# Late pieces of a filter's forward transform in three fp16 products, and a new order at the end of a prologue

## The chip, the cores and the metric

One Trainium2 chip, of which the program uses one core. The metric is the device time of one execution in microseconds (us), as the median of several runs.

## The reference

Two independent computations on 2048 x 448 inputs, whose results stand side by side. A is attention with 16 query heads of 28 columns and one head of keys and values. B is a filter: a real 2D FFT over rows and columns, a product with complex weights, and the inverse FFT.

```python
q = (x @ wq).reshape(B, S, 16, 28).transpose(0, 2, 1, 3)
k, v = x @ wk, x @ wv
p = softmax(einsum("bhqd,bkd->bhqk", q, k) * 28 ** -0.5)
a = einsum("bhqk,bkd->bhqd", p, v).transpose(0, 2, 1, 3).reshape(B, S, 448) @ wo
b = irfft2(rfft2(x) * (w_r + 1j * w_i), s=(S, D))
return concatenate([a, b], axis=-1)
```

## The kernel before

**Prologue** (lines 230 to 720). The projections of A, and the first part of the filter for pieces 0 to 4. Its tasks are given to a planner (`Plan`, line 45) that puts each engine's tasks in an order by their costs and due times; PE's tasks keep the order in which they are written. At its end PE does, in written order, the features of piece 4 (`fa_task(4, 0)`), a small product for the largest bound (`tops`), transposes of half of the values (`first_values`), the products of piece 3 (`fm_task(3)`), and `last_values` (line 628): a register load of `bits` on every engine, the second features unit of piece 4, and the other transposes. Behind it stands a branch on that register (line 646), whose body isn't run with these inputs.

**Main loop** (from line 1280). 256 steps: 16 groups (4 chunks of 512 queries by 4 groups of 4 heads) by 16 blocks of 128 keys. `scores` does half a step, eight fp16 matmuls into two PSUM banks (line 1258) and one exp of 128 x 1024 on ACT (line 1261); `values` does one step, four fp32 matmuls (line 1277; the profile counts an fp32 matmul as two). Three pairs of banks serve the scores, so PE can be up to three score groups ahead of ACT, and up to nine exps may lie ahead of the values. Banks 6 and 7 take the values of one group in turn; the other one of the two is free for other products, the fillers. At a group's end DVE evicts its bank (`group_out`, line 1148).

**Fillers.** What else PE has to do stands in four queues (`work`): late pieces of the filter ("l"), the filter's last part ("z"), output products of A ("w", "more"). `filler` and `fill` put one into the loop when its share is owed. DVE's own work is put in order by a clock that the kernel keeps while it is being written (`after`, `vector`): an event is written out when that clock reaches it. All this is settled before the program runs. On the chip each engine works its list in order and waits for what it needs.

**Late pieces.** The forward transform is cut into 8 pieces of 256 columns (two of them units p = 0, 1). Pieces 5 to 7 are done in the main loop, and the second half of piece 4. For each piece DVE folds its input (`late_fold`, three parts), PE does two features units (`late_features`, 16 fp32 matmuls of 32 x 113 at line 173), DVE copies each out of PSUM (line 1013), PE does two points units (`late_points`, 8 fp32 matmuls of 32 x 226 at line 1026), DVE copies them to `bs` (line 1035), and SP stores them to DRAM (line 196). The inputs of piece 7 are loaded when piece 6 has left their place. When piece 7 is stored, `spectrum` begins the rest of the filter: transform, weights and inverse on DVE, then the z products on PE.

**Round trips.** A largest value over all partitions is found by a store of 128 columns to DRAM and a load of all of them to every partition (`bounce`, line 909: `md`, `mw`). Before the change there are two, one for scales of values and output weights (`largest`), one for the filter's spectrum.

**Queues.** SP issues the loads of inputs, the query copies (`qd`, `qa`), the stores of `bs` and the round trips, in order; POOL issues bulk loads (`wo`, filter weights `w`, `X`) and each group's sums (`sd`, `rs`, `rd`, `R`), also in order. An issue whose source or place isn't ready holds up all that stand behind it.

Of the kernel before, what the change touches and what calls it, by code (L numbers as in the profile page):

```python
# [23 lines left out]
S, D, H = 2048, 448, 16  # L24
# [20 lines left out]
class Plan:  # L45
# [56 lines left out]
def kernel(ctx: ExitStack, tc: tile.TileContext, t: dict):  # L102
# [29 lines left out]
    def spin(*dims):  # L132
        return view(bank[next(turn) % 6], *dims)

    L = 4
# [2 lines left out]
    late["w", 4] = spare[0][1][:, 1416:1928]  # L138
    for q in range(5, 8):
        (one, two), o = spare[q > 5], 452 * (q > 5)  # L140
        late["x", q], late["f", q] = one[:, :1024], one[:, 1024:]
        late["w", q], late["a", q] = two[:, o:o + 512], two[:, o + 512:o + 1416]
    for (n, q), x in late.items():
        dims = {"x": dict(k=4, n=256), "f": dict(k=4, j=4, h=2, m=32), "w": dict(h=2, j=4, m=64), "a": dict(j=2, e=2, n=226)}[n]
        late[n, q] = x.rearrange(f"p ({' '.join(dims)}) -> p {' '.join(dims)}", **dims)
    xb, ff = {}, {}
    f1 = [None]

# [15 lines left out]

    at1 = {}

    def features(pa, f, p):
        for e in range(2):
            for k in range(2):
                for h in range(2):  # L170
                    for r in range(2):
                        r0 = 64 * h + 32 * r
                        mm(pa[r0:r0 + 32, e, 113 * k:113 * k + 113], f[:113, 2 * r + k, 2 * p + e, h], cs1[:113, 2 * r + k],  # L173
                           start=True, stop=True)
# [23 lines left out]

    def late_load(q, names):
        for n in names:  # L200
            nc.sync.dma_start(late[n, q], t["xb"][q] if n == "x" else t["fz"][:, q - L])

    qa, qd = {}, {}

# [27 lines left out]
    with tc.tile_pool(name="f1", bufs=2) as f1[0], tc.tile_pool(name="w1", bufs=1) as w1, ExitStack() as ctx1:  # L232
# [232 lines left out]
            xb_load(q)  # L465

        def late_start():
            late_load(5, "xw")
            late_load(6, "xw")
# [149 lines left out]
        def tops():  # L619
            pb = small["t"] = spin(128)  # L620
            mm(pb[0:1], cmax, cons["ident"], start=True, stop=True)
        bt_ = small_bank(0.2, tops, 0.15, lambda: nc.vector.tensor_reduce(bits, small["t"][0:1], axis=AX.X, op=ALU.max),
                         cm, ident_)
        tv = add(PE, 0.6, first_values, users[-6], ident_, *krow_, *fetched["v"][:7])
        users.append(None)
        fm_task(3)

        def last_values():
            small["rv"] = nc.values_load(bits.bitcast(I32)[0:1, 0:1])
# [105 lines left out]
    def after(when, dur, f, *a):  # L735
        heapq.heappush(events, (when, next(serial), dur, f, a))
# [169 lines left out]
        V.tensor_reduce(m[:, 1:2], peaks[:, 8:16], axis=AX.X, op=ALU.max)  # L906
        bounce(m, fix_peak)

    def bounce(m, then):
        d = dp.tile([128, 2], F32, name="md", bufs=2)  # L910
        nc.sync.dma_start(d, m[:, :2])
        w = ap.tile([128, 128, 2], F32, name="mw", bufs=1)
        nc.sync.dma_start(w, d.rearrange("(o a) b -> o a b", o=1).to_broadcast([128, 128, 2]))

        def go():
            V.tensor_reduce(m[:, :2], w.rearrange("p a b -> p b a"), axis=AX.X, op=ALU.max)
            V.tensor_scalar(m[:, :2], m[:, :2], 1e-30, None, op0=ALU.max)
            then(m)
        after(clk["dve"] + 14.0, 1.0, go)

    def fix_peak(m):
        V.reciprocal(m[:, 2:4], m[:, :2])
# [70 lines left out]
    last_kind = ["w"]  # L993
    done = [0.0]

    def late_fold(q, part=0):
        fold_part(late["x", q][:113], late["f", q][:113], part)
        if part < 2:
            after(clk["dve"], (1.22, 1.4)[part], late_fold, q, part + 1)
        else:  # L1000
            if q == 6:
                late_load(7, "x")
            work["l"].extend([late_features(q, 0), late_features(q, 1)])

    def late_features(q, p):
        def go(b):
            features(view(bank[b], 2, 226), late["f", q], p)
            after(clk["pe"] + LAG, 0.6, out, b)
            if q < 7 and p:
                after(clk["pe"] + (1.8 if q == 5 else 5.0), 1.22, late_fold, q + 1)  # L1010

        def out(b):
            V.tensor_copy(late["a", q][:, p], view(bank[b], 2, 226))
            free[b] = clk["dve"] + 0.1
            after(clk["dve"] + 0.2, 0.0, work["l"].appendleft, late_points(q, p))
        return 0.86, go

    bsl = {}

    def late_points(q, p):  # L1020
        def go(b):
            pb = view(bank[b], 2, 226)
            for h in range(2):
                for e in range(2):
                    for m in (0, 32):
                        mm(pb[64 * e + m:64 * e + m + 32, h], late["w", q][:, h, 2 * p + e, m:m + 32], late["a", q][:, p, e],  # L1026
                           start=True, stop=True)
            after(clk["pe"] + LAG, 0.6, out, b)
            if q == 6 and p:
                late_load(7, "w")  # L1030

        def out(b):
            if p == 0:
                bsl[q] = fp.tile([128, 2, 2, 2, 113], F32, name="bs")
            V.tensor_copy(bsl[q][:, :, :, p], view(bank[b], 2, 2, 113))  # L1035
# [7 lines left out]
        return 0.76, go  # L1043

    def spectrum():
        t0 = clk["dve"] + 3.0
# [334 lines left out]
def _constants():  # L1381
    f = np.float32
    c = {}
    c["krow"] = np.ones((8, S))
    c["krow"][:4], c["krow"][4:] = -ROW, UP
    sel = np.zeros((128, 2, 128))
    blk = np.zeros((128, 128))
    for i in range(4):
        for d in range(DH):
            sel[32 * (d // 4 % 4) + DH + d % 4, d // 16, 32 * i + d] = 1.0  # L1390
        blk[32 * i:32 * i + DH, 32 * i + DH:32 * i + 32] = 0.25 / ROW
    c["mask"] = (np.arange(128) % 32 < DH).astype(f)[:, None]
# [30 lines left out]
    c["fw"], c["fz"] = fw[:, :16], fz.reshape(128, 4, 2, 4, 64)  # L1423
    c["fi"] = np.stack([rot(2 * np.pi * (np.outer(kp, n1) / 64 + n2 * kp[:, None] / S)) for n2 in range(32)], 1)
    c = {k: np.ascontiguousarray(v.astype(f)) for k, v in c.items()}
    for k, scale in (("fi", 64.0), ("cs3", 32.0 * D)):
        x = c[k] * f(scale)
        h = x.astype(np.float16)
        c[k] = np.ascontiguousarray(np.stack([h, (x - h.astype(f)).astype(np.float16)], 2))
    return c  # L1430


# [65 lines left out]
```

## Time and profile before

| | |
|---|---|
| median of 3 runs | 579.47 us (578.97 to 580.06) |
| the profiled execution | 579.57 us, span 577.8 |
| first scores of the main loop | 61.87 us |
| last output products begin | 564.3 us |
| granted TensorE clock | 1.0 |

Times within the profile count from the span's start. "PE" rows are matmuls, "PEld" their weight loads; a row of the timeline merges instructions of one kind that follow each other, gives start and length (the last one's tail included, so the next row's start says when PE went on), and in brackets what ended an idle time. In a group's row the two numbers behind the bar are the busy time and the mean of one in ns.

### The profile page before, as it was taken

The page shows a single profiled execution, that of the slowest core. Times are in us where ns is not written, and L with a number is a line of the kernel's source. Part 1 is how long each engine was busy: PE and PEld are TensorE (multiplying, and loading weights), DVE is VectorE, ACT ScalarE, POOL GpSimd, SP SyncE. Part 2 cuts the span into 40 slices and gives each one's busy share as a digit, 9 for nine tenths or more (in the row PEclk, how much of TensorE's full clock was granted, in tenths as well). Part 3 has the DMA queues.
Part 4 walks back from the last instruction along what each step waited for, and adds up shares of the span by engine and source line. Part 5 has one row for each costly group of instructions (what it writes and reads, how often), then busy time and mean ns, then how long its engine had stood idle before and what let it go on. Part 6 is the DMA issues. An engine that isn't in the chain of part 4 may idle for free.

```text
span 577.8 us, 20635 instructions
## 1 busy us (share of the span) xinstructions
PE 571.3 (99%) x8941; PEld 300.6 (52%) x8941; DVE 390.5 (68%) x747; ACT 513.3 (89%) x580; POOL 110.5 (19%) x199
## 2 busy tenths in 40 slices
PE   9999999999999999999999999999999999999997
PEld 7877454545554444444444444445455555555554
DVE  5996727955421999998998887854366743366544
ACT  4744899999999999999999999998999887899982
POOL 1023311212103012121201311123202321011110
PEclk9999999999999999999999999999999999999999
DMA  8864682625417102243301120457224341212111
GB/s 290 295 205 140 175 247 73 191 81 146 161 37 218 58 18 66 75 123 98 91 34 57 41 60 31 155 208 230 78 88 128 109 130 70 89 58 73 41 55 65
DMA packets 38502, 66.27 MB, mean 115 GB/s; under 512 B 7013, under 2 KB 28653, under 8 KB 38401
## 3 DMA queue, kind: packets, MB, share of 16 engines
q1 hardware_dynamic: 29576, 38.95, 21.1%
q0 software_dynamic: 8688, 25.76, 14.2%
q8 instruction: 70, 1.15, 0.8%
q14 instruction: 24, 0.19, 0.1%
q10 hardware_dynamic: 144, 0.23, 0.1%
HBM read 44.22 MB, written 19.97 MB: 111 GB/s over the span
## 4 chain that ended last, share of the span: by engine, by line
PE 72%; issue 7%; DVE 5%; DMA 3%; POOL 2%; ACT 0%; POOLq 0%; DVEq 0%; ACTq 0%
PE banks L1258 31%; PE banks L1277 30%; PE banks L1196 6%; PE banks L1094 2%; PE banks L1120 2%; DMA rd<-rs 1%; DMA wf<-w 1%; DVE X L817 1%; DVE X L818 1%; PE banks L1026 1%; POOL R L1164 1%; DVE X L859 1%; PE banks L173 0%; ACT yb L1208 0%; DVE w L852 0%
## 5 line engine op out<-in xcount | busy, mean ns | idle before, releaser
L1261 ACT ACTIVATE p<-banks 128x1024 f32<-128x1024 f32 x512 | 477.2, 1094 | 23.7 <-PE banks L1258 22.3
L1258 PE MATMUL banks<-qa,ka 128*32 128x512 f16 x4096 | 276.4, 379 | 0.4 <-PEq L646 0.4
L1277 PE MATMUL banks<-p,vs 128*32 128x512 f32 x2048 | 268.6, 592 | 0.0
L1258 PEld LDWEIGHTS <-ka 128*32 128x32 f16 x4096 | 129.5, 96 | 167.1 <-issue 119.1
L1277 PEld LDWEIGHTS banks<-p,vs 128*32 128x32 f32 x2048 | 69.9, 110 | 43.5 <-issue 1.7
L1156 POOL DMA_DIRECT2D sd<-qraw x15 | 10.1, 671 | 165.4 <-DVE qraw L1151 165.4
L1196 PE MATMUL banks<-woh,o 128*32 128x448 f16 x464 | 39.6, 353 | 0.1
L1164 POOL DMA_DIRECT2D R<-rd x60 | 30.8, 521 | 38.3 <-DMA rd<-rs 38.1
L1196 PEld LDWEIGHTS <-o 128*32 128x32 f16 x720 | 22.6, 97 | 27.4 <-issue 20.2
L859 DVE SCALAR_TENSOR_TENSOR X<-w,X 128x226 f32<-128x226 f32 (+2 forms) x72 | 34.1, 474 | 2.4
L1151 DVE TENSOR_SCALAR qraw<-banks,scales 128x512 f32<-128x512 f32 x15 | 11.3, 750 | 31.5 <-PE banks L1277 31.4
L1201 DVE TENSOR_SCALAR ya<-banks,scales 128x448 f32<-128x448 f32 x12 | 8.2, 683 | 27.5 <-PE banks L1196 27.5
L1127 DVE TENSOR_SCALAR w<-banks,scales 128x256 f32<-128x256 f32 x16 | 7.7, 484 | 27.3 <-PE banks L1120 27.3
L1162 POOL DMA_DIRECT2D rd<-rs x15 | 8.2, 549 | 90.1 <-DVE rs L1161 81.6
L1196 PE MATMUL banks<-wol,o 128*32 128x448 f16 x256 | 24.4, 352 | 0.0
L340 PE MATMUL banks<-xh,wqh 128*128 128x512 f32 x64 | 23.6, 399 | 0.0
L340 PE MATMUL banks<-xh,wql 128*128 128x512 f32 x64 | 23.0, 390 | 0.0
L344 ACT ACTIVATE qraw<-banks 128x512 f32<-128x512 f32 x16 | 9.3, 595 | 15.0 <-PE banks L340 15.0
L817 DVE TENSOR_TENSOR X<-X 128x904 f32<-128x904 f32 (+2 forms) x10 | 9.1, 906 | 16.1 <-DMA X<-t 16.1
L852 DVE SCALAR_TENSOR_TENSOR w<-X 128x113 f32<-128x113 f32 (+2 forms) x56 | 17.8, 356 | 0.1
L1035 DVE COPY bs<-banks 128x452 f32<-128x452 f32 x8 | 5.0, 619 | 18.6 <-PE banks L1026 18.5
L340 PE MATMUL banks<-xl,wqh 128*128 128x512 f32 x48 | 17.3, 390 | 0.0
(157 smaller groups left out, 553.1 us busy)
## 6 DMA issues: line engine op xcount, KB each, us to landing
qa<-qd SPq DMA_DIRECT2D x62, 128.0 KB
ob<-yo SPq DMA_DIRECT2D x16, 256.0 KB
t<-bs SPq DMA_DIRECT2D x16, 226.0 KB
w<-w POOLq DMA_DIRECT2D x8, 452.0 KB, 4.7
X<-t POOLq DMA_DIRECT2D x8, 452.0 KB, 7.1
wf<-w POOLq DMA_DIRECT2D x8, 452.0 KB, 4.0
x<-t POOLq DMA_DIRECT2D x8, 452.0 KB, 4.4
R<-rd POOLq DMA_DIRECT2D x60, 56.0 KB, 2.1
```

The lines of the kernel that those rows point to most:

```text
L340: mm(pq[c, g], w[:, j, gs], x[:, j], start=(j == 0 and n == 0), stop=(j == 3 and n == 1))
L817: todo(226 * n, lambda: TT(both(a), both(a), both(b), op=ALU.add), at)
L852: STT(out, y, sy, x, op0=ALU.mult, op1=ALU.add if c > 0 else ALU.subtract)
L859: todo(226 * n, lambda d=d, q=q: STT(both(d), t[0].rearrange("p r n f -> p r (n f)"), q, both(a), op0=ALU.mult, op1=ALU.add))
L1094: mm(pz[r, j], fb["c2", q % 2][:, x, e, j, r], fb["fi", q % 2][:, j, f], start=(n == 0), stop=(n == 2))
L1120: mm(py[m:m + 32, k].rearrange("p (j n) -> p j n", j=4), cs3[:w, kind, f, m:m + 32], fb["z", q % 2, e][:w, x, :, 64 * r:64 * r + 64], star ...
L1151: V.tensor_scalar(o, bank[b], scale_v, None, op0=ALU.mult)
L1164: nc.gpsimd.dma_start(R[32 * i:32 * i + DH], rd[i:i + 1].to_broadcast([DH, CW]))
L1196: mm(p[r:r + 32], x[c][:, g, s][:, r:r + 32], w[:, m], start=(g == 0 and n == 0), stop=(g == NG - 1 and n == 2))
L1258: mm(bank[b + h][r], ka[:, k:k + 32], qa[c, g][:, 2 * p + h], start=True, stop=True)
L1261: nc.scalar.activation(pt[i], banks[:, b:b + 2], AF.Exp, scale=SCALE / UP / UP)
L1277: mm(bank[b][32 * i:32 * i + 32], vs[:, kc], pt[2 * st + i // 2][:, i % 2], start=(kc == 0), stop=(kc == 15))
```

## The change

Pieces 5 to 7 get the fp16 form that the filter's last part has: a number x is the sum of a high part in fp16 and a low part, x less the high one, in fp16, and a product of two such numbers is three fp16 products (high by high, high by low, low by high), which are summed in PSUM.

- Constants `cs16` and `fz16` come in both parts from DRAM, scaled by 1024. The folded input is scaled by 4096 over the piece's largest input and split by DVE (`late_split`, two instructions). The features are split as they leave PSUM (two instructions in place of one copy), and the points are scaled back as they leave it.
- The largest inputs of pieces 5 to 7 are found early (`late_top`: three reduces on DVE and a third round trip, of three columns).
- Piece 7's input and weights get places of their own and are loaded at the start of the main loop, as is `cs16`.
- A features unit is 48 fp16 matmuls, a points unit 24. Points that are ready go ahead of other late work in order of coming (`late_ready`). The costs that the kernel's clock knows are changed with them, and the filter weights' largest values are asked for earlier (`weight_top` at 14 in place of 24).
- At the prologue's end `fm_task(3)` stands ahead of `first_values`, and the first half of piece 4's last features unit ahead of the register load.

```diff
+        if q < 7:
+            late["x", q], late["W", q] = one[:, :1024], two[:, o:o + 512]
+        late["f", q], late["A", q] = one[:, 1024:], two[:, o + 512:o + 1416]
+    late["C", 0] = spare[1][1][:, :452]
...
+        fm_task(3)
         tv = add(PE, 0.6, first_values, users[-6], ident_, *krow_, *fetched["v"][:7])
         users.append(None)
-        fm_task(3)
 
         def last_values():
+            pas[4, 1] = spin(2, 226)
+            features(pas[4, 1], ff[4], 1, (0,))
             small["rv"] = nc.values_load(bits.bitcast(I32)[0:1, 0:1])
-            pas[4, 1] = spin(2, 226)
-            features(pas[4, 1], ff[4], 1)
+            features(pas[4, 1], ff[4], 1, (1,))
             turn_values(range(8, 16))
...
+    def late_top(qs):
+        m = ap.tile([128, 8], F32, name="mt", bufs=1)
+        V.memset(m, 0.0)
+        for n, q in enumerate(qs):
+            V.tensor_reduce(m[:113, n:n + 1], late["x", q][:113], axis=AX.XY, op=ALU.max, apply_absolute_value=True)
...
+        bounce(m, fix, 3)
...
+    def late_split(q, n):
+        f, x, scale = late["f", q][:113], late["F", q][:113], tops[q][:113, 0:1]
+        if n == 0:
+            V.tensor_scalar(x[:, 0], f, scale, None, op0=ALU.mult)
+            after(clk["dve"], 1.25, late_split, q, 1)
+        else:
+            STT(x[:, 1], f, scale, x[:, 0], op0=ALU.mult, op1=ALU.subtract)
             work["l"].extend([late_features(q, 0), late_features(q, 1)])
+    THREE = (0, 0), (0, 1), (1, 0)
...
-            features(view(bank[b], 2, 226), late["f", q], p)
-            after(clk["pe"] + LAG, 0.6, out, b)
+                    for n, (x, y) in enumerate(THREE):
+                        for h in range(2):
+                            for r in range(2):
+                                r0 = 64 * h + 32 * r
+                                mm(pa[r0:r0 + 32, e, 113 * k:113 * k + 113], f[:113, x, 2 * r + k, 2 * p + e, h],
+                                   c[:113, 2 * r + k, y], start=(n == 0), stop=(n == 2))
...
-    after(24.0, 0.0, weight_top, 0)
+    after(14.0, 0.0, weight_top, 0)
-    after(3.0, 1.22, late_fold, 5)
-    total = 12 * 2.09 + 32 * 0.67 + 6 * 0.86 + 8 * 0.76
+    late_load(0, "C")
...
+    after(6.0, 3.4, late_top, (5, 6, 7))
+    after(6.1, 1.22, late_fold, 5)
+    total = 12 * 2.09 + 32 * 0.67 + 6 * (0.64 + 0.58) + 2 * 0.76
```

How the change moves instructions, as the two programs are written. Line numbers of the changed kernel are its own (line 173 becomes 183, 1258 becomes 1323, and so on).

PE at the end of the prologue, from the small product for the bound to the branch, before (`spol,f` are features of piece 4, `a,fw` the products of piece 3, `ident,kf` the transposes):

```order
L621 MATMUL banks<-ident,cmax 1x128
L606 MATMUL banks<-ident,kf 128x32 x8
L183 MATMUL banks<-a,fw 64x226 x8
L629 TENSOR_LOAD bits
L173 MATMUL banks<-spol,f 32x113 x16
L606 MATMUL banks<-ident,kf 128x32 x8
L646 COMPARE_AND_BRANCH
```

and of the change:

```order
L632 MATMUL banks<-ident,cmax 1x128
L193 MATMUL banks<-a,fw 64x226 x8
L617 MATMUL banks<-ident,kf 128x32 x8
L183 MATMUL banks<-spol,f 32x113 x8
L642 TENSOR_LOAD bits
L183 MATMUL banks<-spol,f 32x113 x8
L617 MATMUL banks<-ident,kf 128x32 x8
L658 COMPARE_AND_BRANCH
```

The products of piece 3 and the transposes have changed places, and eight of the features' matmuls stand ahead of the register load.

SP at the start of the main loop, behind the copies of the keys, before (`qd` and `qa` are the queries of the next group, `md` and `mw` the round trip, `t` the stores of piece 4):

```order
L215 DMA qd<-qh 128x512
L215 DMA qd<-ql 128x512
L218 DMA qa_79<-qd 32x4x512 x4
L911 DMA md<-m 128x2
L913 DMA mw<-md 128x256
L196 DMA t_83<-bs 256x1x226 x2
```

and of the change:

```order
L212 DMA spol<-cs 128x904
L212 DMA x_976<-xb 128x1024
L212 DMA W_978<-fz 128x1024
L226 DMA qd<-qh 128x512
L226 DMA qd<-ql 128x512
L229 DMA qa_79<-qd 32x4x512 x4
L923 DMA md_1092<-mt 128x3
L925 DMA mw<-md_1092 128x384
L923 DMA md_1158<-m 128x2
L925 DMA mw<-md_1158 128x128x2
L206 DMA t_83<-bs 256x1x226 x2
```

Three loads (the constants, piece 7's input and its weights) stand ahead of the queries, and the round trip of the largest inputs ahead of the one that was there.

DVE around the eviction of group 0's bank (`qraw<-banks`), before (`wo` are output weights, `qt`, `qh`, `ql` the next queries, `spol<-banks` the copy of a features unit):

```order
L768 TENSOR_SCALAR woh<-wo,scales 128x448
L770 SCALAR_TENSOR_TENSOR wol<-wo,scales,woh 128x448
L893 TENSOR_REDUCE peaks<-w 128x1
L1151 TENSOR_SCALAR qraw<-banks,scales 128x512
L207 TENSOR_SCALAR qt<-qraw,mask,cvec 128x512
L208 CAST qh<-qt 128x512
L209 TENSOR_TENSOR ql<-qt,qh 128x512
L768 TENSOR_SCALAR woh<-wo,scales 128x448
L770 SCALAR_TENSOR_TENSOR wol<-wo,scales,woh 128x448
L1013 COPY spol<-banks 128x452
```

and of the change (the first row is the low part of piece 5; the small instructions behind the second round trip stand right ahead of it):

```order
L1044 SCALAR_TENSOR_TENSOR spoh<-spoh,t_1357 113x1024
L780 TENSOR_SCALAR woh<-wo,scales 128x448
L782 SCALAR_TENSOR_TENSOR wol<-wo,scales,woh 128x448
L218 TENSOR_SCALAR qt<-qraw,mask,cvec 128x512
L219 CAST qh<-qt 128x512
L220 TENSOR_TENSOR ql<-qt,qh 128x512
L1216 TENSOR_SCALAR qraw<-banks,scales 128x512
L780 TENSOR_SCALAR woh<-wo,scales 128x448
L782 SCALAR_TENSOR_TENSOR wol<-wo,scales,woh 128x448
L905 TENSOR_REDUCE peaks<-w 128x1
L1067 TENSOR_SCALAR spol<-banks 128x452
L1068 SCALAR_TENSOR_TENSOR spol<-banks,spol 128x452
```

The eviction now stands behind the low part of piece 5 and behind the next queries, which followed it.

On PE the features units of pieces 5 to 7 stood after steps 7 and 17, 22 and 33, 37 and 50, and now stand after 18 and 19, 28 and 34, 39 and 50; their points after 11 and 19, 26 and 33, 41 and 53, and now after 20 and 22, 33 and 36, 41 and 51. The points of piece 4 stay after 0 and 4. From step 83 on (now 84) the output and z products follow in almost the same order as before.

More of the change, by code (lines that the diff above doesn't have):

```diff
@@ L140, with shaped @@
         (one, two), o = spare[q > 5], 452 * (q > 5)
[L141 to L144, printed above, removed]
+        if q < 7:
+            late["x", q], late["W", q] = one[:, :1024], two[:, o:o + 512]
+        late["f", q], late["A", q] = one[:, 1024:], two[:, o + 512:o + 1416]
+    late["C", 0] = spare[1][1][:, :452]
+    def shaped(n, q, x):
+        dims = {"x": dict(k=4, n=256), "f": dict(k=4, j=4, h=2, m=32), "w": dict(h=2, j=4, m=64), "a": dict(j=2, e=2, n=226),
+                "F": dict(x=2, k=4, j=4, h=2, m=32), "W": dict(h=2, x=2, j=4, m=64), "A": dict(j=2, x=2, e=2, n=226),
+                "C": dict(k=4, x=2, n=113)}[n]
+        if n == "x" and q > L:
+            shaped("F", q, x)
+        x = x.bitcast(F16) if n in "FWAC" else x
         late[n, q] = x.rearrange(f"p ({' '.join(dims)}) -> p {' '.join(dims)}", **dims)
+    for (n, q), x in list(late.items()):
+        shaped(n, q, x)
     xb, ff = {}, {}
@@ L165, with features @@
     at1 = {}
-    def features(pa, f, p):
-        for e in range(2):
+    def features(pa, f, p, es=(0, 1)):
+        for e in es:
             for k in range(2):
@@ L200, in late_load @@
         for n in names:
-            nc.sync.dma_start(late[n, q], t["xb"][q] if n == "x" else t["fz"][:, q - L])
+            src = t["xb"][q] if n == "x" else t["fz16"][:, q - L - 1] if n == "W" else t["fz" if n == "w" else "cs16"]
+            nc.sync.dma_start(late[n, q], src)
     qa, qd = {}, {}
@@ L994, with fix @@
     done = [0.0]
+    tops = {}
+    def late_top(qs):
[3 more added lines that the diff above has]
+            V.tensor_reduce(m[:113, n:n + 1], late["x", q][:113], axis=AX.XY, op=ALU.max, apply_absolute_value=True)
+        def fix(m):
+            for n, q in enumerate(qs):
+                tops[q] = ap.tile([128, 2], F32, name=f"t{q}", bufs=1)
+                V.tensor_scalar(tops[q][:, 1:2], m[:, n:n + 1], 1.0 / ROW, None, op0=ALU.mult)
+                V.reciprocal(m[:, 4:5], m[:, n:n + 1])
+                V.tensor_scalar(tops[q][:, 0:1], m[:, 4:5], 4096.0, None, op0=ALU.mult)
+                if q in folded:
+                    after(clk["dve"], 0.75, late_split, q, 0)
+        bounce(m, fix, 3)
+    folded = set()
     def late_fold(q, part=0):
@@ L1000, in late_fold @@
         else:
-            if q == 6:
-                late_load(7, "x")
+            folded.add(q)
+            if q in tops:
+                after(clk["dve"], 0.75, late_split, q, 0)
+    def late_split(q, n):
[5 more added lines that the diff above has]
+            STT(x[:, 1], f, scale, x[:, 0], op0=ALU.mult, op1=ALU.subtract)
@@ L1003, in late_fold @@
             work["l"].extend([late_features(q, 0), late_features(q, 1)])
+    THREE = (0, 0), (0, 1), (1, 0)
     def late_features(q, p):
         def go(b):
-            features(view(bank[b], 2, 226), late["f", q], p)
-            after(clk["pe"] + LAG, 0.6, out, b)
+            pa, f, c = view(bank[b], 2, 226), late["F", q], late["C", 0]
+            for e in range(2):
+                for k in range(2):
+                    for n, (x, y) in enumerate(THREE):
[4 more added lines that the diff above has]
+                                   c[:113, 2 * r + k, y], start=(n == 0), stop=(n == 2))
+            after(clk["pe"] + LAG, 1.3, out, b)
@@ L1009, in go @@
             if q < 7 and p:
-                after(clk["pe"] + (1.8 if q == 5 else 5.0), 1.22, late_fold, q + 1)
+                after(clk["pe"] + 1.8, 1.22, late_fold, q + 1)
         def out(b):
-            V.tensor_copy(late["a", q][:, p], view(bank[b], 2, 226))
+            a, pa = late["A", q][:, p], view(bank[b], 2, 226)
+            k = 2.0 ** -17
+            V.tensor_scalar(a[:, 0], pa, k, None, op0=ALU.mult)
+            STT(a[:, 1], pa, k, a[:, 0], op0=ALU.mult, op1=ALU.subtract)
             free[b] = clk["dve"] + 0.1
-            after(clk["dve"] + 0.2, 0.0, work["l"].appendleft, late_points(q, p))
@@ L1016, in late_features, with late_ready @@
-        return 0.86, go
-    bsl = {}
+            after(clk["dve"] + 0.2, 0.0, late_ready, q, p)
+        return 0.64, go
+    def late_ready(q, p):
+        work["l"].insert(len(points), late_points(q, p))
+        points.append((q, p))
+    bsl, points = {}, []
     def late_points(q, p):
         def go(b):
+            if q > L:
+                points.remove((q, p))
             pb = view(bank[b], 2, 226)
             for h in range(2):
[L1024 to L1027, printed above, removed]
+                for n, (x, y) in enumerate(THREE if q > L else ((0, 0),)):
+                    for e in range(2):
+                        for m in (0, 32):
+                            w, a = ((late["W", q][:, h, x], late["A", q][:, p, y]) if q > L else
+                                    (late["w", q][:, h], late["a", q][:, p]))
+                            mm(pb[64 * e + m:64 * e + m + 32, h], w[:, 2 * p + e, m:m + 32], a[:, e],
+                               start=(n == 0), stop=(n == 2 or q == L))
@@ L1034, in out @@
                 bsl[q] = fp.tile([128, 2, 2, 2, 113], F32, name="bs")
-            V.tensor_copy(bsl[q][:, :, :, p], view(bank[b], 2, 2, 113))
+            y, pb = bsl[q][:, :, :, p], view(bank[b], 2, 2, 113)
+            if q > L:
+                V.tensor_scalar(y, pb, tops[q][:, 1:2], None, op0=ALU.mult)
+            else:
+                V.tensor_copy(y, pb)
             free[b] = clk["dve"] + 0.1
@@ L1042, in out @@
                     after(clk["dve"] + 0.1, 0.0, spectrum)
-        return 0.76, go
+        return 0.58 if q > L else 0.76, go
     def spectrum():
```

32 lines of the change are left out of this document (17 added, 15 removed).

## The prediction

> **What bounds the kernel now.** I read the page's table of engines, then the windows by stage, then ACT's waits in each stage, then PE's timeline.
>
> ```profile
> PE 571.3 (99%) x8941; PEld 300.6 (52%) x8941; DVE 390.5 (68%) x747; ACT 513.3 (89%) x580; POOL 110.5 (19%) x199
> ```
>
> PE is never out of work by this count, and ACT's exps fill most of the span too. A busy PE may still stand and wait inside a group, so the next view cuts the main loop where its character changes. Columns: window, its length, then busy time and instructions of PE, PEld, DVE, ACT, POOL.
>
> ```profile
> 61.87:168.90 107.03, 107.00 (x1656) 54.07 (x1657) 64.09 (x107) 103.12 (x112) 20.60 (x38) 1.00 0.48 140
> 168.90:223.07 54.17, 54.06 (x724) 22.65 (x720) 37.26 (x62) 54.17 (x60) 12.55 (x23) 1.00 0.33 98
> 223.07:390.60 167.53, 167.53 (x2428) 77.52 (x2421) 143.04 (x312) 166.45 (x182) 30.88 (x55) 1.00 0.28 87
> 390.60:562.40 171.80, 171.80 (x3344) 92.19 (x3340) 91.47 (x155) 153.45 (x162) 31.59 (x54) 1.00 0.29 96
> ```
>
> The late pieces stand in the first stage. There ACT lacks little, in the second and third next to nothing, and only the last is plainly PE's. ACT's waits in the first and in the last stage:
>
> ```profile
> ACT p L1261 <- PE banks L1258: 4.1, 10, 1.3
> ACT p L1261 <- PE banks L1258: 18.1, 38, 1.9
> ```
>
> So whatever the change does to the late pieces can bring at most 4.1 us in their own stage. Next PE's timeline, rows from several windows:
>
> ```profile
> 77.45 0.96 PE L173 MATMUL banks<-spol,spoh 113*32 113x113 f32 x32
> 78.23 1.48 PE L1258 MATMUL banks<-qa,ka 128*32 128x512 f16 x24
> ...
> 85.12 0.95 PE L1026 MATMUL banks<-spol 128*32 128x226 f32 x16
> 85.88 1.48 PE L1258 MATMUL banks<-qa,ka 128*32 128x512 f16 x24
> ...
> 88.47 1.04 PE L1277 MATMUL banks<-p,vs 128*32 128x512 f32 x8
> ...
> 90.19 1.04 PE L1277 MATMUL banks<-p,vs 128*32 128x512 f32 x8
> ...
> 94.49 1.14 PE L1258 MATMUL banks<-qa,ka 128*32 128x512 f16 x16
> 95.44 1.04 PE L1277 MATMUL banks<-p,vs 128*32 128x512 f32 x8
> ...
> 184.96 1.04 PE L1277 MATMUL banks<-p,vs 128*32 128x512 f32 x8
> ...
> 186.79 1.04 PE L1277 MATMUL banks<-p,vs 128*32 128x512 f32 x8
> ...
> 402.97 0.86 PE L1094 MATMUL banks<-fi,c 128*32 128x128 f16 x48
> 403.64 1.05 PE L1258 MATMUL banks<-qa,ka 128*32 128x512 f16 x16
> ...
> 422.63 0.84 PE L1120 MATMUL banks<-z,cs 113*32 113x256 f16 x24
> 423.29 1.05 PE L1258 MATMUL banks<-qa,ka 128*32 128x512 f16 x16
> ```
>
> From start to start: a step without other work takes PE 1.72 us (88.47 to 90.19), and 1.83 where PE waits for exps to free banks (184.96 to 186.79). So ACT's pace is 1.83 a step and PE gains 0.11 in each step that has nothing else. A features unit costs 0.78 (77.45 to 78.23), a points unit 0.76. After the one at 85.12 PE waits again first at 94.49, five steps on (that score pair takes 0.95 and not 0.86): the lead that PE can have is some 5 x 0.11 = 0.6 us deep. A unit that is longer than the lead makes ACT wait for the rest; a step in which the lead is full makes PE wait. PE's groups follow one another without gaps, so the loop's time is **PE's work plus PE's waits**, and the sum goes by that.
>
> **The change, part by part.** All against the profiled run, 579.57 us (span 577.8), which is 0.1 above the median of 579.47.
>
> *Products.* A features unit goes from 16 fp32 matmuls of 113 columns to 48 fp16 ones. The nearest row is the unit at 402.97: 48 fp16 matmuls of 128 columns in 0.67 us, so 113/128 of it, 0.60 (between 0.59 and 0.67). A points unit goes from 8 of 226 to 24 in fp16; 24 of 256 take 0.66 (422.63 to 423.29), so 0.58. Pieces 5 to 7 have six of each: 6 x 0.18 + 6 x 0.18 = **-2.2 us**. The two points units of piece 4 stay fp32.
>
> *A wait that goes.* The first product of piece 7:
>
> ```profile
> 136.51 1.22 PE L173 MATMUL banks<-spol,spoh 113*32 113x113 f32 x29
> ...
> 137.65 1.47 PE L1258 MATMUL banks<-qa,ka 128*32 128x512 f16 x23
> ```
>
> 1.14 and not 0.78: it waited for the fold on DVE. **-0.3**; whether a new wait takes its place is below.
>
> *PE's waits for exps.* No late product now stands between steps 4 and 18. The lead is full by step 9, and nine steps wait 0.11 each: +0.9. In steps 18 to 53 about -0.1. Behind the last late product the order has 109 score and 51 value groups issued where it had 110 and 53; scores less twice the values are 7 where they were 4, so 1.5 value groups more (1.3 us) fill steps in which PE waited: -1.1. In the six rounds of 16 steps between 84 and 179 the third and fourth group of output products stand two steps apart where they stood three, so one more step per round waits: 6 x 0.11 = +0.65. Together **+0.4**.
>
> *End of the prologue.*
>
> ```profile
> 57.88 0.65 PE L606 MATMUL banks<-ident,kf 32*128 32x32 f32 x8
> 58.46 0.99 PE L183 MATMUL banks<-a,fw 64*64 64x226 f32 x16
> ...
> 59.87 0.98 PE L173 MATMUL banks<-spol,f 113*32 113x113 f32 x32 [0.41 <-issue]
> ...
> 61.87 1.21 PE L1258 MATMUL banks<-qa,ka 128*32 128x512 f16 x16 [0.40 <-PEq L646]
> ```
> ```profile
> L629 POOLq TENSOR_LOAD <-bits x1: 482/482/482, 58.1 to 58.1; - x1
> ...
> L629 PEldq TENSOR_LOAD <-bits x1: 1332/1332/1332, 58.5 to 58.5; - x1
> ```
>
> The register load takes POOL 0.48 and PE 1.33, to 59.8: 0.38 behind the end of the products ahead of it (58.46 + 0.99). It seems to wait until PE is empty, so half of the features put ahead of it delays it by as much (0.39). Fewer instructions are then left to issue before the branch (8 matmuls, about -0.2), and the store products can start as soon as the small product ahead ends, since the four waits of the transposes now pass beside them (about -0.2). **0**, between -0.4 (the load doesn't wait, the 0.41 gap is covered) and +0.3 (only the delay is real).
>
> *DVE, SP and POOL.* Rows for the new DVE work, and for the round trip through DRAM that spreads a largest value:
>
> ```profile
> L1080 DVE TENSOR_SCALAR c<-x,scales 128x904 f16<-128x904 f32 x8 | 5.5, 690 | 9.5 <-PE banks L1094 9.5
> L1081 DVE SCALAR_TENSOR_TENSOR c<-x,scales,c 128x904 f16<-128x904 f32 x8 | 9.3, 1159 | 0.7
> L893 DVE TENSOR_REDUCE peaks<-w 128x1 f32<-128x904 f32 x8 | 8.7, 1087 | 0.0
> L893 DVE TENSOR_REDUCE peaks<-X 128x1 f32<-128x1808 f32 x2 | 4.0, 2002 | 0.0
> L1013 DVE COPY spol<-banks 128x452 f32<-128x452 f32 x6 | 3.7, 624 | 8.5 <-PE banks L173 8.5
> ...
> 74.03 0.34 SPq L911 DMA_DIRECT2D md<-m  x1
> 85.74 0.34 SPq L913 DMA_DIRECT2D mw<-md  x1
> 89.05 0.44 DVE L916 TENSOR_REDUCE m<-mw 128x2 f32<-128x256 f32 x1 [2.23 <-DMA mw<-md]
> 72.43 1.59 POOL L802 DMA_DIRECT2D X<-t  x3
> 99.87 0.54 POOL L765 DMA_DIRECT2D wo<-wo  x1
> wo<-wo POOLq DMA_DIRECT2D x2, 224.0 KB, 4.7
> ```
>
> By size: three reduces 3 x 1.23, three splits 3 x (0.78 + 1.31), six second evictions 6 x 0.62, some 12 small ones of 0.17: 16 us more on DVE, which has 64.1 of the first stage's 107.0 busy. It fits; the question is when. The order has two tight places.
>
> First, step 18. The first features unit needs bank 7, which group 0's eviction frees. On DVE that now stands behind both round trips: 2.0 (some eleven small ones), 1.3 (low part), 1.1 (a weight split), 1.7 (the next queries) and 0.75 for itself, 6.8 in all. PE arrives at about 97.3 (step 16's scores at 94.49, less some 0.8 that ACT no longer waits in group 0, plus two steps), so the second trip must end by **90.5**. In before the only one took from 74.03 to 89.05, since its store landed 11.7 us later, with the bulk that POOL issues around 72.4. Now the first store goes at about 75.5, behind the loads of piece 7. The bulk goes later too, at 76 to 80, since it waits for DVE's reduces that now follow piece 7's. So the first store should land ahead of it, and the second trip end at 88 to 90. I take 0; the other end is a rival.
>
> Second, step 28, the first product of piece 6. From the end of the product of step 19 PE has 19 score and 9 value groups and two points units ahead of it: 19 x 0.43 + 9 x 0.86 + 1.2 = 17.1 us. DVE has to evict (0.25 + 1.25), then the 21 instructions up to piece 6's low part: 2 x 2.0 for X, 2 x 1.09, 2.1 for the split, and 16 of 0.25 to 0.69 for folds, copies and weights, some 16.4, or 1.2 less where they overlap. That is 16.7 to 17.9. It may also wait for the third weight load, issued at 99.87 and 4.7 us on its way. So 0 to 2; I take **+0.4**, near the lower end, since a wait there is over before the next group's queries. Piece 7's product at step 39 comes out level.
>
> The transforms on DVE and the z products behind them hang on loads at 176 to 187 behind POOL's sums of group 2; those don't move. Cost 0.
>
> Sum: -2.2 - 0.3 + 0.4 + 0 + 0.4 = -1.7: **577.9 us**.
>
> **Rivals.**
>
> *The late inputs eat the gain.* Both tight places at their middle, 1.5 us of PE standing still: 577.9 - 0.4 + 1.5 = 579.0. For it: piece 7 waited for its fold in before, and DVE now has 80 of 107 us there. Against: the new order already puts the units of pieces 5 and 6 some steps later.
>
> *Slower: the second round trip is late.* SP issues the four transfers in order, so the second trip starts only behind the first one's landing. If the first store lands with the end of POOL's bulk, as the one of 74.03 did, that is some 12 us from 76, 88; the first load comes 3.3 later (85.74 to 89.05), and the second trip, two landings of about 2 us on, at 94 to 96: 3.5 to 5.5 past the 90.5 from which it decides. Every us past it is a us that PE stands at step 18, since the unit itself uses up the lead. 577.9 + 3.5 to 5.5 = 581.4 to 583.4. Against: the bulk has moved behind the store. The Trainium skill, page "DMA: Bandwidth & Descriptors", section "Queues, rings and completion order", has the engines take turns between queues packet by packet, by which 1 KB wouldn't wait out another queue's loads; 11.7 us here speaks against leaning on it.
>
> *Slower: small matmuls have a floor.* If each fp16 matmul took a slot of its own of 25 ns, features would take 48 x 0.025 = 1.2 and points 0.6: 6 x 0.42 - 6 x 0.16 = +1.6 in place of -2.2, 581.7. The row at 402.97 has 48 of them in 0.67, 14 ns each, over four column groups, which speaks against it at 128 columns; 113 is near. The Trainium skill has this floor ("TensorE: Matmul & The Clock Gate", section "Wait — 56ns, not 53.3ns?"), for matmuls one after the other in one array.
>
> **How the numbers follow.** Forecast 0.58 (576.9 to 578.3, by the prologue's bounds and stalls of 0 to 0.8), late inputs 0.28 (578.3 to 580.4), late round trip 0.10, floor 0.04. About 0.2%, 1.16 us, is what a measurement of this kernel tells from no change. Faster by more: the forecast and little else, 0.59. Within: 0.28. Slower, over 580.6: the last two, 0.13. The range leaves out the slower mechanisms and little below: 576.9 to 580.4.
>
> **What would show it.** Right: features units of 0.60 and points of 0.58 between scores; ACT's wait in the first stage down from 4.1 to about 1.5; steps 9 to 18 at 1.83. The prologue: first scores at 61.6 to 62.1. Wrong: a features unit of over 0.7 with a DVE releaser at step 18 or 28, a second round trip that ends after 90.5, or output products at step 84 that wait for DVE.

## The result, and the profile after

The changed kernel takes **655.12 us** (median of 6 runs, 652.91 to 656.73) where the kernel before takes 579.88 (578.97 to 580.06): ratio 1.130, 95% interval 1.1284 to 1.1315. The forecast was 577.9. The profiled run of the changed kernel is the one of 652.91.

The page first, of the kernel before and then of the changed one: the line that counts packets, and of the changed one the span, the engines' busy time and the granted TensorE clock in 40 slices.

```profile
DMA packets 38502, 66.27 MB, mean 115 GB/s; under 512 B 7013, under 2 KB 28653, under 8 KB 38401
```
```profile
span 651.1 us, 20948 instructions
...
PE 577.0 (89%) x9085; PEld 297.2 (46%) x9085; DVE 405.7 (62%) x774; ACT 513.8 (79%) x580; POOL 109.9 (17%) x199
...
PEclk9999996559999989598999999999999999999999
...
DMA packets 71447, 66.74 MB, mean 102 GB/s; under 512 B 39956, under 2 KB 61596, under 8 KB 71344
```

PE is as busy as before (577.0 us, 571.3 before) in a span that is 73 us longer, so PE stood still; the two dips of its clock say where. And 33,000 packets are new, all of them under 512 B, for 0.5 MB more. The windows of the changed kernel (window, length, busy time and instructions of PE, PEld, DVE, ACT, POOL, then clock, DMA share, GB/s) and its waits:

```profile
97.80:139.60 41.80, 0.21 (x4) 0.00 (x0) 6.33 (x18) 1.43 (x2) 0.00 (x0) 0.56 0.24 18
139.60:231.00 91.40, 91.35 (x1580) 45.58 (x1583) 53.75 (x82) 87.42 (x96) 20.54 (x38) 0.98 0.39 103
231.00:300.00 69.00, 43.69 (x524) 19.58 (x520) 42.27 (x69) 38.86 (x42) 7.44 (x13) 0.80 0.26 61
```
```profile
PE banks L1058 <- DVE qraw L1216: 41.6, 1, 41.6
DVE m L928 <- DMA mw<-md: 40.5, 1, 40.5
...
DVE X L829 <- DMA wf<-w: 30.4, 1, 30.4
```

PE does nothing for 41.8 us and misses another 25.3 of 69 later. Both waits of the first hole are one chain: PE's first features unit waits for the eviction of group 0's bank, and that stands on DVE behind `m`, which waits for the load of the second round trip. The timeline of the changed kernel, SP's round trips, DVE's reduces of them, and PE's first late products:

```profile
80.37 0.34 SPq L925 DMA_DIRECT2D mw<-md  x1
80.76 1.13 SPq L923 DMA_DIRECT2D md<-m  x1
90.71 0.38 SPq L925 DMA_DIRECT2D mw<-md  x1
...
215.57 0.39 SPq L925 DMA_DIRECT2D mw<-md  x1
...
88.54 0.75 DVE L928 TENSOR_REDUCE mt<-mw 128x3 f32<-128x384 f32 x1 [6.17 <-DMA mw<-md]
132.89 0.49 DVE L928 TENSOR_REDUCE m<-mw 128x2 f32<-128x256 f32 x1 [40.52 <-DMA mw<-md]
...
262.02 0.49 DVE L928 TENSOR_REDUCE mx<-mw 128x2 f32<-128x256 f32 x1 [16.25 <-DMA mw<-md]
...
139.65 1.33 PE L1058 MATMUL banks<-spol,spoh 113*32 113x113 f16 x48 [41.65 <-DVE qraw L1216]
140.75 2.80 PE L1323 MATMUL banks<-qa,ka 128*32 128x512 f16 x24
```

Three loads spread a largest value to all partitions. The one of three columns is there 8 us after its issue (80.37 to 88.54). The two of two columns take 42 us (90.71 to 132.89) and 46 us (215.57 to 262.02); the only one that the prediction quoted, of the kernel before, took 3.3. What differs is the target. `bounce` now makes a tile of three columns for all trips and takes the first two for two (`[:, :, :cols]`), so each partition is written as 128 pairs with a gap behind each. The rows of SP shown with the change have it: `mw<-md_1158 128x128x2` where the kernel before has `mw<-md 128x256`. A partition's 1 KB, one packet, becomes 128 packets of 8 B: 128 x 128 = 16,384 in place of 128, twice.

### The profile page after: what moved, and what is told of

Read it like the earlier page. It is cut to its first block, busy times and chain, and to the rows that moved or that the text cites. A ratio compares the mean times of both kernels' runs of the same rounds, so it can differ in the third digit from the quotient of the medians.

```text
span 651.1 us, 20948 instructions
## 1 busy us (share of the span) xinstructions
PE 577.0 (89%) x9085; PEld 297.2 (46%) x9085; DVE 405.7 (62%) x774; ACT 513.8 (79%) x580; POOL 109.9 (17%) x199
## 4 chain that ended last, share of the span: by engine, by line
PE 67%; DMA 18%; DVE 3%; issue 1%; ACT 0%; POOL 0%; SPq 0%; DVEq 0%; ACTq 0%
PE banks L1323 29%; PE banks L1342 28%; DMA mw<-md 14%; PE banks L1261 5%; PE banks L1159 2%; PE banks L1185 2%; DMA md<-m 2%; DMA x<-xb 1%; DMA md<-mx 1%; PE banks L1058 1%; PE banks L1090 1%; DMA qa<-qd 0%; DMA o<-lows 0%; ACT yb L1273 0%; DVE m L794 0%
## 5 line engine op out<-in xcount | busy, mean ns | idle before, releaser
L1323 PE MATMUL banks<-qa,ka 128*32 128x512 f16 x4096 | 281.5, 384 | 16.4 <-DMA qa<-qd 10.6
L1342 PE MATMUL banks<-p,vs 128*32 128x512 f32 x2048 | 272.8, 599 | 0.0
L1058 PE MATMUL banks<-spol,spoh 113*32 113x113 f16 x192 | 3.7, 235 | 41.6 <-DVE qraw L1216 41.6
L1261 PEld LDWEIGHTS <-o 128*32 128x32 f16 x720 | 21.0, 97 | 37.0 <-issue 28.0
L829 DVE TENSOR_TENSOR X<-X 128x904 f32<-128x904 f32 (+2 forms) x10 | 9.1, 905 | 30.4 <-DMA wf<-w 30.4
L1058 PEld LDWEIGHTS <-spoh 113*32 113x32 f16 x192 | 3.5, 108 | 44.4 <-issue 44.1
```

Source lines behind the costliest of these rows:

```text
L1058: mm(pa[r0:r0 + 32, e, 113 * k:113 * k + 113], f[:113, x, 2 * r + k, 2 * p + e, h], c[:113, 2 * r + k, y], start=(n == 0), stop=(n == 2))
L1261: mm(p[r:r + 32], x[c][:, g, s][:, r:r + 32], w[:, m], start=(g == 0 and n == 0), stop=(g == NG - 1 and n == 2))
L1323: mm(bank[b + h][r], ka[:, k:k + 32], qa[c, g][:, 2 * p + h], start=True, stop=True)
L1342: mm(bank[b][32 * i:32 * i + 32], vs[:, kc], pt[2 * st + i // 2][:, i % 2], start=(kc == 0), stop=(kc == 15))
```

## The experiments

Since the profiled runs reach their first scores at 61.9 to 63.1 us, whatever the kernel, spans are also compared from there: 577.8 - 61.87 = 515.9 before, 651.1 - 62.32 = 588.8 after.

**The gap: taken away, kept for one trip, put into the kernel before.** Four kernels, run together.

```diff
-        w = ap.tile([128, 128, 3], F32, name="mw", bufs=1)[:, :, :cols]
+        w = ap.tile([128, 384], F32, name="mw", bufs=1)[:, :128 * cols].rearrange("p (a b) -> p a b", b=cols)
```

The flat target for all trips (`flat`):

> The change as it is, but the round trips' loads go into one flat stretch of the same place (128x256 for two columns, where the change writes pairs with a gap behind each, 128x128x2). Theory A (each of the two gapped loads is cut into 16,384 packets of 8 bytes and takes some 42 and 46 us; PE and DVE wait for them, and nothing else of the change costs much): both loads take 3 to 5 us, PE's hole from 97.4 to 139.7 goes, 577.9 by the prediction's sum (576.9 to 579.5). Rival B (the round trip is late because four transfers stand in order on SP and the eviction of group 0's bank stands behind them): the hole stays in part, second trip past 90.5, 581 to 600. Rival C (the products or other new work are dearer than priced, and PE's lower clock is part of it): over 600 with the clock still under 1.

Flat, the gap kept for the trip of values and output weights, or for the spectrum's:

> The flat loads of the run above, but the gapped one kept for the round trip of values and output weights (the one at 80 us). Theory A: 16,384 packets more than flat, PE stands from about 97 to 139, so flat + 42 = 620 (615 to 626), with the second disturbance at 232 to 295 gone. If the wait in the first stage is worth less, because group 1's queries would have come late anyway: under 610.

> The flat loads, but the gapped one kept for the spectrum's round trip (the one at 210 us). Theory A: the rest of the loss, 655.1 - 577.9 - 42 = 35, so 613 (605 to 620); PE stands for queries and output products at 232 to 295, since DVE waits 46 us in front of the inverse transform with the bank evictions behind it. Rival (the second disturbance follows from the first hole, which shifts the groups against the spectrum): under 590.

And the kernel before with the gap in its target and nothing else changed:

> The kernel before with nothing changed but the gap in the round trips' load target (both of its trips). Theory A: the gap alone costs what the change lost, two loads of 42 to 46 us in place of 3.3: 579.9 + 70 to 80 = 650 to 660. Rival (only the new order puts a bank eviction behind the trip, before could hide it): under 620.

| | us | ratio to before (95%) | packets |
|---|---|---|---|
| flat | 585.67 | 1.0093 (1.0073 to 1.0112) | 38,935 |
| strided_first | 625.74 | 1.0796 (1.0777 to 1.0814) | 55,191 |
| strided_last | 615.81 | 1.0624 (1.0603 to 1.0646) | 55,191 |
| before_strided | 652.82 | 1.1263 (1.1243 to 1.1282) | 71,013 |

Each gapped load adds 55,191 - 38,935 = 16,256 packets, which is 16,384 less 128. The first costs 40.1 us, the second 30.1; flat and the two prices make 655.9, the changed kernel has 655.1. The rivals to that fall: the kernel before has no cover for the trip either (+73 us), and the second disturbance comes without the first. But flat is not at 577.9: it is 6 us **slower** than the kernel before, so theory A was right about the 70 us and wrong that nothing else costs. Rival B's range, 581 to 600, holds it. Flat's timeline (SP's trips, DVE's reduces and the eviction, PE, and POOL's bulk):

```profile
76.92 0.38 SPq L923 DMA_DIRECT2D md<-mt  x1
80.13 0.34 SPq L925 DMA_DIRECT2D mw<-md  x1
80.52 1.23 SPq L923 DMA_DIRECT2D md<-m  x1
90.28 0.32 SPq L925 DMA_DIRECT2D mw<-md  x1
...
93.69 0.42 DVE L928 TENSOR_REDUCE m<-mw 128x2 f32<-128x256 f32 x1 [2.13 <-DMA mw<-md]
...
99.58 0.74 DVE L1216 TENSOR_SCALAR qraw<-banks,scales 128x512 f32<-128x512 f32 x1
...
100.38 0.80 PE L1058 MATMUL banks<-spol,spoh 113*32 113x113 f16 x48 [2.05 <-DVE qraw L1216]
...
228.67 0.37 PE L1261 MATMUL banks<-woh,o 128*32 128x448 f16 x4 [2.05 <-DVE w L864]
...
79.20 2.12 POOL L814 DMA_DIRECT2D X<-t  x4
...
173.67 1.07 POOL L814 DMA_DIRECT2D X<-t  x2 [7.37 <-DMA t<-bs]
174.73 0.55 POOL L1227 DMA_DIRECT2D rd<-rs  x1
```

The second store of 1 KB waits from 80.52 to 90.28, its load is there at 93.7, 3.2 us past the 90.5 that the prediction named, and PE stands at step 18. From the starts of PE's groups, less the 1.72 of a step and the units' own time, PE waits 4.0 us in steps 17 to 21, 1.1 at step 28 and 2.4 at step 84. The last 1.2 of the 4.0 come by way of POOL: its next `wo` load stands behind group 0's sums, goes out at 105.78, and DVE waits 2.9 us for it (to 108.69) ahead of the copy to `bs` that frees a bank for the next points unit (111.72).

**POOL's bulk and POOL's order.** One move each, and both.

```diff
-        after(30.0 + i, 0.0, spread, i)
+        after(9.0 + i, 0.0, spread, i)
...
-            after(t0 + 1.0 * (i - 4), 0.0, spread, i)
+            after(t0 + 4.0 + 0.1 * (i - 4), 0.0, spread, i)
```

> flat (585.7) with one thing moved: POOL's four first X loads (452 KB each) are issued ahead of the weights' and output weights' loads, at about 66 us, and no longer at 79 to 81, right on top of the two round trips. Theory D (the second store waits from 80.5 to 90.3 because it stands in one queue behind the first trip's load of 192 KB, which shares the DMA engines with 3.2 MB of bulk): the first trip lands at 83 to 85 in place of 87.7, the second at 88 to 90.5 in place of 93.7, and PE's waits at steps 17, 18 and 21 (2.2, 0.5 and 1.2 in flat) fall to 1 us or less together: 582 to 583. Theory E (it is the order of four transfers on SP by itself that makes the second trip late, whatever else is on its way): the second trip still ends past 93, 585 to 586.

> flat with one thing moved: POOL's X loads of pieces 6 and 7 stand all four behind group 2's rd and R, where flat has two of them ahead, which wait 7.4 us for the stores of piece 7 and hold rd up (169.6 in the kernel before, 174.7 in flat). Theory F (the transforms on DVE start 5.3 us later for it, at 190.8 against 185.5, and PE's wait of 2.4 us at step 84 is for them): they start at 186 to 187, the wait at step 84 goes to 0.5 or less, 583.3 to 584. Rival (the transforms hang on the loop's own delay in the first stage): they start past 189, 585 to 586.

> Both moves together on flat. Theories D and F: the second round trip lands by 90.5 and the transforms start by 185, so that of the 8 us by which flat stands above the prediction's sum only the prologue (0.4 to 0.8) and the wait at step 28 (1.1 in flat) are left: 579.5 to 581, level with the kernel before or 0.2% above it. If the gains don't add (less wait at one place gives a full lead and waits for exps behind it): 582 to 583.

`early_bulk` missed: 587.01 (1.0125, 1.0110 to 1.0141), no faster than flat. Its timeline of SP shows why:

```profile
80.07 1.78 SPq L229 DMA_DIRECT2D qa<-qd  x4
81.95 0.39 SPq L923 DMA_DIRECT2D md<-mt  x1
88.42 0.34 SPq L925 DMA_DIRECT2D mw<-md  x1
88.81 0.42 SPq L923 DMA_DIRECT2D md<-m  x1
92.90 0.32 SPq L925 DMA_DIRECT2D mw<-md  x1
```

Bulk at 66 us holds up the queries (`qd`, stored at about 67), whose copies wait until 80.07 (73.83 in flat), and both trips stand behind them on SP. The second store, now clear of bulk, takes 4.1 us and not 9.8; the first, now beside the weights' loads of 78.6 to 80.7, takes 6.5 and not 3.2. So the transfer that meets the bulk pays, whichever it is, and the series on SP passes it on: theory D has the mechanism, but this move only shifted the collision.

`rd_first` came as expected: 583.42 (1.0066, 1.0051 to 1.0081). The time alone hardly tells it from flat, two of whose six runs took 583.24 and 583.36; the rows do. Its timelines of POOL and DVE, and behind them DVE's first transform in flat and in the kernel before:

```profile
173.01 0.55 POOL L1227 DMA_DIRECT2D rd<-rs  x1 [5.55 <-DVE rs L1226]
...
187.76 1.10 DVE L829 TENSOR_TENSOR X<-X 128x904 f32<-128x904 f32 x1 [15.04 <-DMA X<-t]
```
```profile
190.82 1.10 DVE L829 TENSOR_TENSOR X<-X 128x904 f32<-128x904 f32 x1 [19.16 <-DMA wf<-w]
```
```profile
185.48 1.10 DVE L817 TENSOR_TENSOR X<-X 128x904 f32<-128x904 f32 x1 [16.06 <-DMA X<-t]
```

No wait is left at step 84: the transforms start at 187.8, where flat has 190.8 and the kernel before 185.5, although this run's loop is 0.4 us later than flat's from its first scores on and PE stood longer at step 18 (3.3). That wait cost more than its length. Behind it the granted clock is 0.62 from 101.87 to 106.32, and the features unit, 24 scores and 8 values there take 4.45 us; flat, with its clock at 1.00, takes 2.77 for them from 100.38 on. So, against flat, 2.4 less at step 84, 0.7 less in steps 17 to 21, 0.4 less at step 28 and 1.7 more by the clock make -1.8, and the spans from the first scores differ by -1.8.

`early_rd`, 585.77 (1.0126, 1.0108 to 1.0145), can't be told from `early_bulk` by its ratio. In its rows it has the gain of the one (no wait at step 84) and the loss of the other (5.1 us at step 18, 6.1 in `early_bulk`).

**The prologue in the old order.**

> flat with the prologue's end in the old order (products of piece 3 behind the transposes, the whole features unit behind the register load), nothing else changed. If the new order costs what the first scores show (62.64 in flat, 62.32 in the changed kernel, 61.87 before): first scores back at 61.9, 584.9 to 585.3. The prediction's term 0: 585.7. If the new order gains: over 586.

585.20 (1.0095, 1.0077 to 1.0112), which can't be told from flat, but the rows can. PE's timeline, flat and then the old order in it:

```profile
58.12 0.38 PE L632 MATMUL banks<-ident,cmax 128*1 128x128 f32 x2
...
62.64 1.00 PE L1323 MATMUL banks<-qa,ka 128*32 128x512 f16 x12 [0.40 <-PEq L658]
```
```profile
58.26 0.38 PE L632 MATMUL banks<-ident,cmax 128*1 128x128 f32 x2
...
62.75 0.78 PE L1322 MATMUL banks<-qa,ka 128*32 128x512 f16 x8 [0.41 <-PEq L657]
```

From the bound's product to the first scores: 4.52 in the new order, 4.49 in the old (4.51 in the kernel before, 61.87 - 57.36). The edit is worth nothing; later first scores come from ahead of it.

**The third trip: left out, out of series, clear of bulk.** `notop_rd` computes with a constant scale and searches no largest inputs. `mfirst_rd` puts the old trip's reduces ahead of the new one's, and issues the two stores, then the two loads. The last two move the four first X loads from POOL to SP, behind the trips (on `rd_first`, and on `mfirst_rd`). The edits, in this order:

```diff
-            V.tensor_reduce(m[:113, n:n + 1], late["x", q][:113], axis=AX.XY, op=ALU.max, apply_absolute_value=True)
+        V.memset(m, 8.0)
-        bounce(m, fix, 3)
+        after(clk["dve"] + 14.0, 3.0, fix, m)
...
-            bounce(m, fix)
+            bounce(m, fix, hold=True)
-    after(6.0, 3.4, late_top, (5, 6, 7))
+    after(10.0, 3.4, late_top, (5, 6, 7))
...
-        nc.gpsimd.dma_start(X[:, r, n0:n0 + 8], t1v[r, :, n0:n0 + 8])
+        (nc.sync if i < 4 else nc.gpsimd).dma_start(X[:, r, n0:n0 + 8], t1v[r, :, n0:n0 + 8])
```

> rd_first (583.4) without the search for the largest inputs of pieces 5 to 7: the three reduces and the third round trip are left out and the scale is a constant; everything else, the splits and the fp16 products too, stands in the same order. Theory G (the prediction's sum holds, and what flat had above it is the second trip in series with the first, and POOL's order): the one trip left lands by 89.5, PE's waits at steps 17 to 21 (5 us in rd_first) go, features 0.61 and points 0.58 stay, and the time is 578 to 579.5, under the kernel before. Rival H (the new DVE work, the splits and second evictions, makes the stage too tight by itself): waits of 2 us or more stay between steps 17 and 30, 580.5 to 582.

> rd_first with the round trips taken out of series: the reduces and the store of the trip for values and output weights stand ahead of those of the largest inputs, both stores are issued one behind the other, then both loads, each into a place of its own; on DVE the eviction of group 0's bank no longer stands behind the trip of the largest inputs and piece 5's low part. Theory G: both stores land by 86, the loads by 89 and 91, group 0's bank is evicted by 95, PE's waits at steps 17 to 21 fall under 1 us: 578.5 to 580. Rival I (the bulk on POOL holds up the stores all the same, some 12 us as in the kernel before): loads at 92 and 94, the first features unit waits 1 to 3 us for its split: 581 to 583.

> rd_first (583.4), the trips in series as in the change, but the four first X loads (1.8 MB) are issued by SP behind the round trips and not by POOL on top of them (nothing is put ahead of the queries, which is what made early_bulk later). Theory D (bulk that is on its way makes each small transfer late): the mt store lands in some 4 us and its load by 86, the second store in 3 to 5 us in place of 10.5, its load by 91; PE's waits at steps 17 to 21 fall from 5.0 to 1 us or less, 579 to 580.5. Theory E (the series by itself): second load past 93, 582 to 584.

> mfirst_rd (581.3) with the same X loads on SP behind both trips. Theory D: of the bulk ahead of the stores only the weights' and output weights' 1.35 MB is left, the stores land by 81 in place of 86.9, the loads by 84 and 86, the split of piece 5 is done by 95 and the wait of 1.5 us at step 19 goes: 578.5 to 579.8, level with or under the kernel before (579.8). If the first features unit or the bank's eviction still waits: 580.5 or more.

| | us | ratio to before (95%) | span from first scores | second store, issue to next issue |
|---|---|---|---|---|
| kernel before | | | 515.9 | |
| flat | 585.67 | 1.0093 | 521.3 | 9.8 |
| rd_first | 583.42 | 1.0066 | 519.5 | 10.5 |
| xsp_rd | 580.74 | 1.0016 (1.0004 to 1.0027) | 517.8 | 6.7 |
| mfirst_rd | 581.34 | 1.0034 (1.0022 to 1.0047) | 517.1 | in parallel |
| notop_rd | 579.13 | 0.9988 (0.9979 to 0.9997) | 515.2 | none |
| xsp_mfirst_rd | 579.19 | 0.9985 (0.9976 to 0.9994) | 515.0 | in parallel |

The rows of `notop_rd` (SP's one trip, and PE at step 18):

```profile
75.37 0.44 SPq L923 DMA_DIRECT2D md<-m  x1
87.53 0.34 SPq L925 DMA_DIRECT2D mw<-md  x1
...
97.74 1.04 PE L1340 MATMUL banks<-p,vs 128*32 128x512 f32 x8
98.60 0.80 PE L1056 MATMUL banks<-spol,spoh 113*32 113x113 f16 x48
```

Theory G holds: without the trip the unit at step 18 starts right behind the values ahead of it, and the time is just under the kernel before. H falls with that. What goes is a little more than the trip: its three reduces on DVE go too, and POOL's bulk starts 5.5 us earlier for it (71.56, in flat 77.08). The one store takes 12.2 us (75.37 to 87.53) beside that bulk, with no load of another trip ahead of it; in the kernel before it took 11.7. So the bulk alone makes a store late.

For `mfirst_rd`, rival I is the nearer: the stores wait for the bulk as before, the first features unit for its split. Its timeline (SP, PE), and the same places once the X loads are out of the way:

```profile
75.98 0.77 SPq L924 DMA_DIRECT2D md<-m  x1
77.64 0.56 SPq L924 DMA_DIRECT2D md<-mt  x1
86.90 0.80 SPq L928 DMA_DIRECT2D mw<-md  x2
...
102.38 0.69 PE L1066 MATMUL banks<-spol,spoh 113*32 113x113 f16 x40 [1.33 <-DVE spoh L1052]
```
```profile
75.58 0.81 SPq L924 DMA_DIRECT2D md<-m  x1
77.66 0.34 SPq L924 DMA_DIRECT2D md<-mt  x1
82.19 0.80 SPq L928 DMA_DIRECT2D mw<-md  x2
...
100.94 0.80 PE L1066 MATMUL banks<-spol,spoh 113*32 113x113 f16 x48
101.55 0.62 PE L1331 MATMUL banks<-qa,ka 128*32 128x512 f16 x8
```

10.9 us from store to load become 6.6, and the unit waits for nothing. D's numbers were a little bold here (82.2 and not 81), and for `xsp_rd` half missed: the second load goes out at 87.67, PE still waits 2.2 us for the eviction at step 18, and 580.74 lies just past D's 580.5. Here too the clock falls behind the wait (0.62 from 99.68 to 104.13), and the same three groups take 4.45 us; that 1.7 is in its 517.8. Bulk and series both count. `xsp_mfirst_rd` computes all that the change computes and is, with `notop_rd`, the fastest of these, 0.15% under the kernel before.

## Why the prediction was wrong

**The step that failed** is the price of the round trips. The prediction had "the first load comes 3.3 later (85.74 to 89.05)" from a row of the kernel before, gave the second trip "two landings of about 2 us", so its load about 2, and took "0; the other end is a rival". The change rewrote the target of that very load, in its diff and in the rows of SP shown with it; the shape was read as a size. At 42 us for it, the place was right: step 18, the eviction of group 0's bank behind the second trip, decided at 90.5, but the rival there was priced at 3.5 to 5.5 and not at 40. The spectrum's trip, the same function called from code that the change doesn't touch, got no term; it cost 30.

**Two smaller steps failed** below that, as flat shows, where the sum said -1.7 and the span from the first scores grew by 5.3.

- "So the first store should land ahead of it, and the second trip end at 88 to 90." The first half came (76.92 to 80.13); the second store then met the bulk, and the trip ended at 94.1. The rival "the second round trip is late" has what flat does in place and size, 4.0 us of waits at steps 17 to 21 against 3.5 to 5.5, but by another transfer: it let the first store wait out the bulk, and in flat the second one does.
- "those don't move. Cost 0", of the transforms that hang on loads at 176 to 187. POOL's order had changed there: two X loads stand ahead of group 2's `rd` and hold it until piece 7's stores have landed. 2.4 us at step 84.

**The rest of the sum held.** Terms as predicted, and in flat:

| | predicted | flat |
|---|---|---|
| features unit, points unit | 0.60, 0.58 | 0.61 (103.67 to 104.28), 0.58 (106.43 to 107.01) |
| twelve products | -2.2 | -2.1 |
| wait for piece 7's fold | -0.3 | -0.3 |
| PE's waits, steps 9 to 17 | +0.9 | +0.9 |
| behind the last late product | -1.1 | -1.1 |
| rounds of output products | +0.65 | +0.6 |
| prologue's end | 0 | 0.0 |
| step 28 | 0 to 2, took 0.4 | 1.1 |
| second trip, steps 17 to 21 | 0 | 4.0 |
| transforms, step 84 | 0 | 2.1 |

The last row is 2.4 less the 0.3 that PE waited there before. The last three rows are 7.2 where the sum had 0.4: -1.7 - 0.4 + 7.2 = 5.1, beside 5.3 measured. ACT's wait in the first stage, said to fall from 4.1 to about 1.5, is 6.8 in flat and 2.6 in `xsp_mfirst_rd`. The floor of 25 ns for small matmuls did not appear: 48 in 0.61 us are 13 ns each. The rule of the Trainium skill that the prediction set aside, turns between queues packet by packet ("DMA: Bandwidth & Descriptors", section "Queues, rings and completion order"), was rightly not leaned on: 1 KB took 9.8 us in flat beside the bulk, behind 192 KB of its own queue, and 12.2 in `notop_rd` beside it without these 192 KB.

Why `notop_rd` is 0.7 us under the kernel before and not 1.7 isn't settled. In its profiled run the clock was granted at 0.56 from 62.08 to 66.00, where the kernel before had 1.00, and the first 24 scores take 2.49 us (62.08 to 64.57) and not 1.47 (61.87 to 63.34), about 1 us more. The profiled runs of `early_rd` and `strided_last` have the same dip (0.58 and 0.59 from 61.92 to 66.00), the others none. But `xsp_mfirst_rd`, which has none, is no further under the kernel before, so that isn't all of it.

## What to carry to other kernels

Price a DMA by the shape on both its sides, and read its row in the changed program before taking a duration from the old one: a slice that leaves a gap in the target turns each row into as many packets as it has runs. A helper that the diff edits is changed for all its callers. A small transfer that something waits for is late by what bulk is on its way and by what stands ahead of it in its queue; in `xsp_mfirst_rd`, out of series and with 1.8 MB of the bulk behind it, PE waits for it no longer.

## What was not expected of the hardware

The 16,384 packets of 8 B took 42 us, about 2.6 ns each, while the DMA engines were far from busy (share 0.24 in the hole, 18 GB/s). The Trainium skill says that one descriptor moves one contiguous run of the last dimension ("DMA: Bandwidth & Descriptors", section "Why a DMA increments its semaphore by 16 and not by 1"); the profile counts packets, and its 16,256 more for each gapped load, one for each run, agree.

They also slowed what other queues had on their way. Issues with KB and median us to landing, the changed kernel from 216 to 262 us:

```profile
X<-t POOLq DMA_DIRECT2D x2, 452.0 KB, 16.2
wf<-w POOLq DMA_DIRECT2D x2, 452.0 KB, 17.6
R<-rd POOLq DMA_DIRECT2D x4, 56.0 KB, 15.0
```

The same issues in flat (178 to 200 us) take 5.2, 6.4 and 2.8. So DVE's wait for `wf`, 19.2 us in flat, is 30.4 in the changed kernel, and then DVE stands 16.2 more for the gapped load itself.

And PE paid after the hole as well: with the clock at 0.56 in it and at 0.50 from 139.65 to 143.00, the first features unit took 1.10 us (139.65 to 140.75) where the next took 0.61 (144.39 to 145.00). Much shorter waits had that price too: behind 3.3 us at step 18 in `rd_first` and 2.2 in `xsp_rd` the clock was 0.62 for 4.45 us, behind 2.2 in flat it stayed at 1.00. Why one wait of 2.2 us has it and the other not, no run here shows.
